# Attention and a feed-forward network on one core: the value products of eight more pairs on 64x64 quarters, in another place of the order

## The chip, the core and the metric

The kernel runs on one core of a Trainium2 chip. The core has a matrix engine (TensorE, PE in the profile, with a separate row PEld for its weight loads), a vector engine (VectorE, DVE), a scalar engine (ScalarE, ACT), GpSimd (POOL) and SyncE (SP), which here only issues DMAs. Each engine works through its own list of instructions in order, and semaphores tie the lists together. The time is the device time of one launch in microseconds (us). The kernel before takes 794.22 us, the median of 3 runs (794.18 to 794.61).

## What is computed

First attention within chunks of 64 tokens, for 8 batches, 8 heads, 576 tokens and a head width of 64; then a feed-forward layer over all 4608 tokens of width 512, with an inner width of 2048:

```python
q_c, k_c, v_c = (t.reshape(B, H, nc, 64, D) for t in (q, k, v))
scores = np.matmul(q_c, k_c.transpose(0, 1, 2, 4, 3)) / np.sqrt(D)
attn = np.exp(scores - np.max(scores, axis=-1, keepdims=True))
attn = attn / (np.sum(attn, axis=-1, keepdims=True) + 1e-09)
x = np.matmul(attn, v_c)   # then transposed to (4608, 512)
h = x @ w_in               # (4608, 2048)
out = (h - np.tanh(h)) @ w_out
```

## The kernel before

The tokens are worked through in 36 pairs of 64-token chunks, p = 0 to 35, each with its 8 heads. Four pairs (512 tokens) make a group of the feed-forward layer; there are nine groups, g = 0 to 8. All float32 numbers are split into a high and a low part, so that a product is three matmuls (high by high, high by low, low by high). From group 1 on the parts are float16.

For a pair p of 8 or more the attention is a chain through all engines. SP loads query and key (`load`) and the values (`load_values`, into one of four places of `rawv`, p % 4). DVE takes the largest value (`largest`, "tops" in the rows), POOL reduces it over partitions once a group, and a power of two follows. ACT and DVE then write the values' high and low float16 part (`split_high` L349, `split_low` L353). PE makes the scores as 16 matmuls of 64x64 (`scores`, `quarters` L183); DVE takes their maximum and subtracts it (`less` L374, L378), ACT the exponential, DVE the sum and the shares, which are split (L405, L410) and turned by a DMA transpose (`turned` L415). PE multiplies the turned shares by the values (`products`). `results` writes the outcome into the input of the feed-forward layer, 3 steps for an even p and 9 for an odd one: first ACT copies the accumulator out (L450), then ACT and DVE make sums and differences (L460 to L465) and their high and low parts (L454).

Products have two forms here. For p = 8 to 15 the values stand block-diagonally in tiles padded with zeros, and `products` runs 24 matmuls with a 128x128 weight tile (L440) into the second of two accumulator banks. For p = 16 and more `crossed_products` runs 48 matmuls of 64x64 on the four quarters of the array (L427), into the upper halves of both banks. Padded tiles exist in two places, p % 2. `two_banks` gives a new accumulator pair each time (there is one buffer) until `third`; after that one pair, `att.banks`, is kept, and its first bank is also the feed-forward bank Z.

The feed-forward layer of groups 2 and later uses a scheme with 7 products for 8 (`Winograd`). Its first matrix product is made in banks X, Y and Z (`product`, L687, 12 matmuls of 128x256 each), each result goes through ACT and DVE (`copied`, `summed` L709, `tanh` L713, `less` L717, `high` L723, `low` L727) and becomes a chunk g of two float16 halves. The second matrix product takes one chunk at a time (`chunk` L746, 12 matmuls of 128x512). The third matmul of a chunk is the first that reads the low half. The same holds for groups 0 and 1 with `gemm1` (L575), `tanh`, `less`, `high`, `low` (L584 to L608) and `gemm2` (L620).

The order is written out by hand for all engines in two tables of tokens, PLAN and SECOND. SECOND covers pairs 8 to 15 and groups 1 and 2. Its tokens that matter here: S8 is the scores of pair 8, m its `less`, E its exponentials, z, h, l its shares and their parts, t its transpose, s and d the split of its values, V8 its products, X8.0 to X8.8 the steps of `results`, u its `largest`. G and P are `gemm1` and `gemm2`, K5 is chunk 5 of group 2, gx, gy, gz and so on are products into banks X, Y, Z, and st, sn, su, sh, sl are `summed` to `low`. From group 3 on only PE's order is given by hand (the loops at the end of the function: scores of pair p + 1 directly behind the products of p); a scheduler places the other engines' work and may place it ahead of the last instructions of SECOND. In the text below K14 is the third chunk that PE works off after the scores of pair 16.

Of the kernel before, what the change touches and what calls it, by code (L numbers as in the profile page):

```python
# [10 lines left out]
F32 = mybir.dt.float32  # L11
# [5 lines left out]
AF = mybir.ActivationFunctionType  # L17
ALU = mybir.AluOpType
# [14 lines left out]
FIRST = tuple(sum(SIZES[:g]) for g in range(len(SIZES)))  # L33
# [28 lines left out]
CROSSED = FIRST[LATER + 1]  # L62

@with_exitstack
def attn_ffn_kernel(ctx: ExitStack, tc: tile.TileContext, qkE, vE, qL, kL, vL, w_in, w_out, out):
# [212 lines left out]
    class Late:  # L278
# [2 lines left out]


        def __init__(self, pool):
            self.pool, self.st, self.banks = pool, defaultdict(dict), None

            self.rawv = pool.tile([P, MOST // P, H * CH], F32, name="rawv", bufs=1)
            self.v16, self.a, self.aT, self.blocks = [], [], [], []
            self.room([pool.tile([P, 2, DM], F16, name=f"v16{a}", bufs=1).rearrange("p a n -> p (a n)") for a in "hl"])

        def two_banks(self):  # L290

            return ps_a.tile([P, 2, 4 * P], F32, name="psa") if self.banks is None else self.banks

        def room(self, v):

            self.v16.append([t.rearrange("p (c hp d) -> p c hp d", c=2, hp=4) for t in v])
            for t in v:
                nc.gpsimd.memset(t, 0.0)

        def load(self, p):  # L300
            if p < NPAIR:
# [27 lines left out]
            power(self.st[f"g{g}"]["across"], to, back)  # L329
            to_x[g], from_x[g] = to, back  # L330

        def crossed(self, p):
            return p >= CROSSED

        def split_parts(self, p):
            to = to_x[p // 4]
            if self.crossed(p):
                vh, vl = (t.rearrange("p c hp d -> p (c hp d)")[:, :DM] for t in self.v16[p % len(self.v16)])
                yield vh, vl, self.rawv[:, p % 4], to
                return  # L340
            v = self.rawv[:, p % 4].rearrange("p (a d) -> p a d", d=D)
            vh, vl = (t.rearrange("p c hp d -> p (c hp) d") for t in self.v16[p % len(self.v16)])
            for u in range(2):
                r = slice(u * D, (u + 1) * D)
                yield vh[r, :, r], vl[r, :, r], v[r], to[r]

        def split_high(self, p):
            for h, l, v, to in self.split_parts(p):
                nc.scalar.activation(h, v, AF.Copy, scale=to)  # L349

        def split_low(self, p):
            for h, l, v, to in self.split_parts(p):
                nc.vector.scalar_tensor_tensor(out=l, in0=v, scalar=to, in1=h, op0=ALU.mult, op1=ALU.subtract)  # L353

        def split(self, p):
            self.split_high(p)
# [73 lines left out]
        def products(self, p):  # L430
            if self.crossed(p):
                return self.crossed_products(p)
            d = self.st[p]
            bank = d["bank"] = self.two_banks()[:, 1]
            ps = bank.rearrange("p (hp c k) -> p hp c k", hp=4, c=2)
            for hp in range(4):
                for c in range(2):
                    cs = slice(c * CH, (c + 1) * CH)
                    for k, (a, b) in enumerate(((0, 0), (0, 1), (1, 0))):
                        nc.tensor.matmul(ps[:, hp, c, :], lhsT=self.v16[p % len(self.v16)][a][:, c, hp, :], rhs=d["a16"][:, b, hp, cs], start=(k == 0), stop=(k == 2))  # L440

        def results(self, p, x):

# [2 lines left out]
            cs = slice(p % 4 // 2 * P, (p % 4 // 2 + 1) * P)  # L446

            def out(to):
                flat = to.rearrange("p s k (c t) -> p (s k) c t", c=2) if self.crossed(p) else to.rearrange("p s k n -> p (s k n)")
                return lambda: nc.scalar.mul(flat, bank, 2.0 ** -14)  # L450

            def parts(slot, a):
                h, l = (t[:, slot:slot + a.shape[1], :, cs] for t in x)
# [572 lines left out]
```

## Time and profile before

The profile is one execution that took 793.73 us, of which the span of the engines' work is 792.0 us. The median of the timed runs is 794.22 us.

| engine | busy us | share | instructions |
|---|---|---|---|
| PE (matmul) | 784.5 | 99% | 7178 |
| PE (weight load) | 519.5 | 66% | 7178 |
| DVE | 610.8 | 77% | 1114 |
| ACT | 485.3 | 61% | 938 |
| POOL | 47.9 | 6% | 82 |

The granted clock of PE is at nine tenths or more of full speed in all of the 40 slices of the span. DVE's busy share is nine tenths in the slices from the second to the thirteenth (some 20 to 257 us) and six to eight tenths in most of the later ones. The chain that ended last lies with PE for 88% of the span. Busy matmuls overlap, since each is printed with its way through the array; what a matmul costs PE is the distance from its start to the next start. In the same way a DVE or ACT instruction starts some 0.08 us before the printed end of the one ahead if it needs nothing from it. Pairs 8 to 15 are worked on between 130 and 285 us; the groups from 3 on begin at 291 us.

### The profile page before, as it was taken

Reading aid. Unit: us, or ns where it says so; the run is one execution under the profiler, and the core shown is the slowest. Engines: PE = TensorE matmul, PEld = TensorE weight load, DVE = VectorE, ACT = ScalarE, POOL = GpSimd, SP = SyncE. Lnnn points to the kernel's source line nnn. Section 1 sums busy time; section 2 is a strip of 40 time slices with the busy share of each in tenths; the row PEclk is TensorE's granted clock in tenths of the full one; section 3 lists DMA queues with packets and bytes.
Section 4 is the critical chain, followed back from the end, with each engine's and each line's share of the span. In section 5 each row is a group of like instructions: output and inputs, shape, how many; then the busy total and the mean of one; then the engine's idle time right before and its main releaser. Section 6 shows DMA issues by size and latency. Waiting matters only on the chain.

```text
span 792.0 us, 17323 instructions
## 1 busy us (share of the span) xinstructions
PE 784.5 (99%) x7178; PEld 519.5 (66%) x7178; DVE 610.8 (77%) x1114; ACT 485.3 (61%) x938; POOL 47.9 (6%) x82
## 2 busy tenths in 40 slices
PE   8999999999999999999999999999999999999998
PEld 4877884444676666666666666666666666666664
DVE  8999999999999997676867686768676777654443
ACT  6989968986675655555645465556455645453443
POOL 0032135500000000000000000000000000000000
PEclk9999999999999999999999999999999999999999
DMA  9887848853131224111311131112211220001001
GB/s 355 321 234 220 222 130 179 150 134 81 28 111 50 81 61 108 47 55 54 108 55 54 55 105 37 50 40 92 68 55 41 68 67 15 15 12 43 1 1 54
DMA packets 58735, 72.43 MB, mean 91 GB/s; under 512 B 32800, under 2 KB 33056, under 8 KB 58528
## 3 DMA queue, kind: packets, MB, share of 16 engines
q1 hardware_dynamic: 53760, 61.81, 24.8%
q0 software_dynamic: 4752, 9.44, 7.0%
q8 instruction: 56, 0.92, 0.5%
q14 instruction: 23, 0.19, 0.1%
q10 hardware_dynamic: 144, 0.07, 0.0%
HBM read 45.09 MB, written 9.44 MB: 69 GB/s over the span
## 4 chain that ended last, share of the span: by engine, by line
PE 88%; DVE 7%; ACT 2%; DMA 2%; issue 1%; SPq 0%; DVEq 0%; ACTq 0%
PE po L746 36%; PE ph L687 23%; PE psa L687 9%; PE po L620 7%; PE ph L575 7%; PE psa L183 2%; PE psa L427 1%; DVE w L153 1%; DVE w L157 1%; DMA raw<-w_out 1%; PE psa L440 1%; DVE wl L164 1%; ACT junk L168 1%; DMA raw<-w_in 1%; DVE w L149 1%
## 5 line engine op out<-in xcount | busy, mean ns | idle before, releaser
L746 PE MATMUL po<-wl,gh 128*128 128x512 f16 x672 | 154.2, 379 | 0.0
L746 PE MATMUL po<-wl,gl 128*128 128x512 f16 (+1 forms) x672 | 151.6, 375 | 0.0
L687 PEld LDWEIGHTS <-wh 128*128 128x128 f16 x1344 | 129.2, 98 | 22.3
L687 PE MATMUL ph<-xh,wl 128*128 128x256 f16 x672 | 114.6, 273 | 0.0
L746 PEld LDWEIGHTS <-gl 128*128 128x128 f16 x720 | 69.1, 98 | 67.3
L687 PEld LDWEIGHTS <-wl 128*128 128x128 f16 x1008 | 98.5, 98 | 21.6
L746 PEld LDWEIGHTS <-gh 128*128 128x128 f16 x672 | 65.7, 98 | 67.3
L687 PE MATMUL ph<-xl,wl 128*128 128x256 f16 x336 | 91.6, 273 | 0.0
L687 PE MATMUL ph<-xh,wh 128*128 128x256 f16 x448 | 76.7, 273 | 0.0
L687 PE MATMUL psa<-xh,wh 128*128 128x256 f16 x448 | 76.4, 273 | 0.0
L620 PE MATMUL po<-wl,gh 128*128 128x512 f16 (+1 forms) x192 | 63.2, 383 | 0.0
L687 PE MATMUL ph<-xl,wh 128*128 128x256 f16 x224 | 61.1, 273 | 0.0
L687 PE MATMUL psa<-xl,wh 128*128 128x256 f16 x224 | 61.0, 273 | 0.0
L713 ACT ACTIVATE t<-t,sig 128x512 f32<-128x512 f32 x37 | 26.6, 719 | 32.9 <-DVE t L709 32.8
L713 ACT ACTIVATE t<-wh,sig 128x512 f32<-128x512 f32 x38 | 27.3, 720 | 31.0 <-DVE wh L709 30.9
L713 ACT ACTIVATE t<-spare,sig 128x512 f32<-128x512 f32 x37 | 26.6, 720 | 30.0 <-DVE spare L709 30.0
L575 PE MATMUL ph<-xl,wl 128*128 128x512 f16 x192 | 43.8, 379 | 0.2 <-DVE t L591 0.2
L454 ACT CAST xh<-wh 128x512 f16<-128x512 f32 (+1 forms) x56 | 31.4, 564 | 11.1 <-DVE wh L461 9.9
L709 DVE TENSOR_TENSOR wh<-ph,wh 128x512 f32<-128x512 f32 x28 | 19.3, 688 | 24.3 <-PE ph L687 24.1
L709 DVE TENSOR_TENSOR t<-ph,t 128x512 f32<-128x512 f32 x28 | 19.2, 687 | 23.4 <-PE ph L687 23.3
L387 ACT ACTIVATE s<-s 128x512 f32<-128x512 f32 x24 | 15.1, 629 | 36.0 <-DVE s L378 36.0
L717 DVE SCALAR_TENSOR_TENSOR wh<-wh,sig,t 128x512 f32<-128x512 f32 x38 | 28.4, 748 | 11.1 <-ACT t L713 11.0
(181 smaller groups left out, 1444.3 us busy)
## 6 DMA issues: line engine op xcount, KB each, us to landing
raw<-w_in SPq DMA_DIRECT2D x16, 512.0 KB, 6.0
raw<-w_out SPq DMA_DIRECT2D x16, 512.0 KB, 6.7
wh<-wl POOLq DMA_DIRECT2D x32, 256.0 KB, 4.2
rawv<-vL SPq DMA_DIRECT2D x28, 256.0 KB, 3.1
rawq<-qL SPq DMA_DIRECT2D x28, 256.0 KB, 3.1
rawk<-kL SPq DMA_DIRECT2D x28, 256.0 KB, 3.5
out<-wh SPq DMA_DIRECT2D x28, 256.0 KB, 2.1
qk<-qkE SPq DMA_DIRECT2D x8, 512.0 KB, 8.7
```

The costliest lines, as they stand in the source:

```text
L149: nc.vector.tensor_single_scalar(w, w, 3, op=ALU.logical_shift_left)
L153: nc.vector.scalar_tensor_tensor(out=w, in0=low, scalar=29, in1=w, op0=ALU.logical_shift_right, op1=ALU.bitwise_or)
L183: nc.tensor.matmul(ps[os, r ^ o if crossed else r, hp * CH:(hp + 1) * CH], lhsT=lhsT(rs, hp, o), rhs=rhs(rs, hp, o), start=True, stop=True)
L387: nc.scalar.activation(s, s, AF.Exp, scale=scale)
L454: return (lambda: nc.scalar.copy(out=h, in_=a)), (lambda: nc.vector.tensor_sub(l, a, h))
L575: nc.tensor.matmul(ph, lhsT=self.weight(fc, 0, a)[:, kc * P:(kc + 1) * P], rhs=x[b][:, kc, cols], start=(k == 0), stop=(k == 3 * KC - 1))
L620: nc.tensor.matmul(self.po[t], lhsT=gg[a][:, ts], rhs=self.weight(fc, 1, b), start=(k == 0), stop=(k == 3 * FC - 1))
L687: nc.tensor.matmul(bank[:, q * 2 * P:(q + 1) * 2 * P], lhsT=self.weight(u, a, i, q, kc), rhs=self.x[j][:, b, kc, :], start=(first and q == ...
L709: nc.vector.tensor_tensor(out=c, in0=self.banks["X"], in1=self.m5 if n % 4 == 3 else c, op=ALU.subtract if n % 4 == 2 else ALU.add)
L713: nc.scalar.activation(t, self.now[n][0], AF.Tanh, scale=self.ff.sig)
L717: nc.vector.scalar_tensor_tensor(out=c, in0=c, scalar=self.ff.sig, in1=t, op0=ALU.mult, op1=ALU.subtract)
L746: nc.tensor.matmul(bank, lhsT=g[a][:, ts], rhs=half_w[1][fc][:, b, columns], start=(first and s == 0 and k == 0), stop=(last and s == 1 an ...
```

## The change

Pairs 8 to 15 use the 64x64 form, too: the padded form, its two zero fills per pair of tiles on POOL and the distinction between the forms go. The split values lie unpadded, so that one tile holds two pairs, and there are four places, p % 4, instead of two. `split_high` and `split_low` are one instruction of 128 partitions each where pairs 8 to 15 had two of 64. In SECOND each V stands directly ahead of the scores of the pair two further on (V8 S10, V9 S11, V11 S12, V12 S13, to V15 S16), V10 stands alone, and the first step of the results (X.0) behind that. The products leave their accumulator pair to the scores that follow (`shared`). The scores and the layout of the values in memory are rearranged to match.

```diff
-... z8 ... T0.3.1 T0.2.0 V8 G8 T0.3.0 ... q10 X8.0 i8 ... C1.12 S10 G2 P10 t9 ...
+... z8 ... T0.3.1 T0.2.0 G8 T0.3.0 ... q10 i8 ... C1.12 V8 S10 X8.0 G2 P10 t9 ...
...
-... rB4 sl11 su12 X13.6 V15 gv3 X14.2 X15.0 X15.1 sh12 st13 ... K11 S16 su13 ...
+... rB4 sl11 su12 X13.6 gv3 X14.2 sh12 st13 gw3 sn13 K11 V15 S16 X15.0 su13 ...
...
         def two_banks(self):
-            return ps_a.tile([P, 2, 4 * P], F32, name="psa") if self.banks is None else self.banks
+            if self.banks is not None:
+                return self.banks
+            t, self.shared = self.shared, None
+            return ps_a.tile([P, 2, 4 * P], F32, name="psa") if t is None else t
         def room(self, v):
-            self.v16.append([t.rearrange("p (c hp d) -> p c hp d", c=2, hp=4) for t in v])
-            for t in v:
-                nc.gpsimd.memset(t, 0.0)
+            self.v16 += zip(*(t.rearrange("p (n k) -> n p k", n=2) for t in v))
...
         def split_parts(self, p):
...
+            return (*self.v16[p % 4], self.rawv[:, p % 4], to_x[p // 4])
...
+        def products(self, p):
+            d = self.st[p]
+            self.shared = None
+            tile_ = self.two_banks()
+            if self.banks is None:
+                self.shared = tile_
+            ps = tile_[:, :, 4 * CH:]
+            v = [t.rearrange("p (c hp d) -> p c hp d", c=2, hp=4) for t in self.v16[p % 4]]
...
-    turned[:, :, CROSSED:, 1] = turned[:, ::-1, CROSSED:, 1]
+    turned[:, :, :, 1] = turned[:, ::-1, :, 1]
```

Three places of the engines' lists show what moves. Line numbers of the changed kernel are smaller by 1 to 21. The first is DVE where pair 15 ends and group 3 begins, from the split of the values of pair 17 on, before:

```order
L353 SCALAR_TENSOR_TENSOR wh_1813<-rawv,to,wh_1812 128x512
L460 TENSOR_TENSOR wh_2168<-wh_2167,wh_2166 128x256
L461 TENSOR_TENSOR wh_2168<-wh_2167,wh_2168 128x256
L709 TENSOR_TENSOR spare<-ph,spare 128x512
L464 TENSOR_TENSOR wh_2169<-wh_2167 128x256
L465 TENSOR_TENSOR wh_2169<-wh_2168,wh_2166 128x256
L454 TENSOR_TENSOR xl<-wh_2168,xh 128x4x128
L717 SCALAR_TENSOR_TENSOR spare<-spare,sig,t 128x512
L727 SCALAR_TENSOR_TENSOR gh<-wh_2713,to_g,gh 128x512
L454 TENSOR_TENSOR xl<-wh_2169,xh 128x4x128
L727 SCALAR_TENSOR_TENSOR gl<-spare,to_g,gl 128x512
L315 TENSOR_REDUCE tops<-rawv 128x1
```

The same place now (the first two rows split pairs 17 and 18, the sixth pair 19; the two L706 rows are the low halves of chunks 12 and 13):

```order
L341 SCALAR_TENSOR_TENSOR v16l<-rawv,to,v16h 128x512
L341 SCALAR_TENSOR_TENSOR wh_1811<-rawv,to,wh_1810 128x512
L696 SCALAR_TENSOR_TENSOR spare<-spare,sig,t 128x512
L706 SCALAR_TENSOR_TENSOR gh<-wh_2794,to_g,gh 128x512
L315 TENSOR_REDUCE tops<-rawv 128x1 x3
L341 SCALAR_TENSOR_TENSOR wh_1811<-rawv,to,wh_1810 128x512
L439 TENSOR_TENSOR wh_2222<-wh_2221,wh_2220 128x256
L440 TENSOR_TENSOR wh_2222<-wh_2221,wh_2222 128x256
L443 TENSOR_TENSOR wh_2223<-wh_2221 128x256
L444 TENSOR_TENSOR wh_2223<-wh_2222,wh_2220 128x256
L706 SCALAR_TENSOR_TENSOR gl<-spare,to_g,gl 128x512
L315 TENSOR_REDUCE tops<-rawv 128x1
```

With four places the scheduler splits pairs 18 and 19 here too, and takes the largest values of pairs 20 to 23 where it took those of 20 and 21. The split of pair 19 uses the place that V15 reads. The sums of pair 15 (L460 to L465 before, L439 to L444 now) have moved from ahead of the two low halves to between them; the remaining rows of group 2 and of the softmax of pair 16 follow behind.

The second place is DVE where pair 11 ends and group 2 begins, before (L608 is the low half for P12, L374 and L378 belong to the softmax of pair 12, L460 to L454 to the results of pair 11):

```order
L460 TENSOR_TENSOR wh_2168<-wh_2167,wh_2166 128x256
L461 TENSOR_TENSOR wh_2168<-wh_2167,wh_2168 128x256
L608 SCALAR_TENSOR_TENSOR gl<-t,to_g,gh 128x512
L374 TENSOR_REDUCE mx<-psa 128x8
L378 TENSOR_TENSOR s<-psa,mx 128x512
L454 TENSOR_TENSOR xl<-wh_2168,xh 128x4x128
```

And the same place now:

```order
L587 SCALAR_TENSOR_TENSOR gl<-t,to_g,gh 128x512
L362 TENSOR_REDUCE mx<-psa 128x8
L366 TENSOR_TENSOR s<-psa,mx 128x512
L439 TENSOR_TENSOR wh_2222<-wh_2221,wh_2220 128x256
L440 TENSOR_TENSOR wh_2222<-wh_2221,wh_2222 128x256
L433 TENSOR_TENSOR xl<-wh_2222,xh 128x4x128
```

The two sums of pair 11 have gone behind the softmax steps, directly ahead of the row (L433) that needs ACT's high part of these sums.

The third place is ACT around the first step of the results of pair 13 (L450, now L429), before:

```order
L723 ACTIVATE gl<-wh_2713,to_g 128x512
L450 ACTIVATE wh_2167<-psa 128x512
L723 ACTIVATE gh<-spare,to_g 128x512
L510 ACTIVATE wh_3098<-wh_2908,to_w 128x512
L713 ACTIVATE t<-t,sig 128x512
```

And now:

```order
L702 ACTIVATE gl<-wh_2794,to_g 128x512
L702 ACTIVATE gh<-spare,to_g 128x512
L489 ACTIVATE wh_3172<-wh_3011,to_w 128x512
L692 ACTIVATE t<-t,sig 128x512
L429 ACTIVATE wh_2221<-psa 128x512
```

The copy out of the accumulator has gone three instructions later, as V13 itself has gone behind a whole chunk on PE.

## Rows read from the trace of the kernel before

**Rows 1.** Who PE waited for, 133 to 792 us: total, times, longest
```profile
PE ph L575 <- DVE t L591: 0.2, 1, 0.2
```

**Rows 2.** Busy time 222 to 285 us: length, PE, PEld, DVE, ACT, POOL; clock, DMA
```profile
222.00:285.00 63.00, 63.00 (x568) 42.37 (x566) 61.07 (x114) 42.30 (x71) 0.79 (x1) 1.00 0.26 76
```

**Rows 3.** PE in order of time at V9 (padded): start, us, line, form
```profile
175.12 0.86 PE L440 MATMUL psa<-s,wh 128*128 128x64 f16 x24
175.82 0.60 PE L620 MATMUL po<-wl,gh 128*128 128x512 f16 x2
```

**Rows 4.** PE in order of time, pair 16: products on quarters, scores, next product
```profile
304.15 0.26 PE L427 MATMUL psa<-wh,v16h 64*64 64x64 f16 x8
...
304.60 0.69 PE L183 MATMUL psa<-rawk,rawq 64*64 64x64 f32 x32
305.23 0.39 PE L687 MATMUL ph<-xh,wh 128*128 128x256 f16 x2
```

**Rows 5.** DVE in order of time, from the sums of pair 11 on
```profile
203.26 0.42 DVE L460 TENSOR_TENSOR wh<-wh,wh 128x256 f32<-128x256 f32 x1
...
204.06 0.75 DVE L608 SCALAR_TENSOR_TENSOR gl<-t,to_g,gh 128x512 f16<-128x512 f32 x1
204.72 0.68 DVE L374 TENSOR_REDUCE mx<-psa 128x8 f32<-128x512 f32 x1
...
206.65 0.15 DVE L123 TENSOR_REDUCE from<-xtop 128x1 f32<-128x4 f32 x1
...
211.30 0.75 DVE L608 SCALAR_TENSOR_TENSOR gl<-t,to_g,gh 128x512 f16<-128x512 f32 x1
```

**Rows 6.** PE in order of time: end of S12, and P11
```profile
204.57 0.60 PE L620 MATMUL po<-wl,gh 128*128 128x512 f16 x2
...
212.38 0.59 PE L620 MATMUL po<-wl,gh 128*128 128x512 f16 x2
```

**Rows 7.** DVE in order of time: softmax of pair 14, low half of chunk 5
```profile
242.89 0.68 DVE L374 TENSOR_REDUCE mx<-psa 128x8 f32<-128x512 f32 x1
...
247.84 0.74 DVE L727 SCALAR_TENSOR_TENSOR gl<-t,to_g,gl 128x512 f16<-128x512 f32 x1
```

**Rows 8.** PE in order of time: S14 and K5
```profile
241.97 0.69 PE L183 MATMUL psa<-rawk,rawq 64*64 64x64 f32 x32
...
249.13 1.24 PE L746 MATMUL po<-wl,gl 128*128 128x512 f16 x5
```

**Rows 9.** PE in order of time: behind V15, second product, S16, K14
```profile
278.59 0.38 PE L687 MATMUL ph<-xh,wh 128*128 128x256 f16 x2
...
279.90 0.38 PE L687 MATMUL ph<-xh,wl 128*128 128x256 f16 x2
...
283.89 0.69 PE L183 MATMUL psa<-rawk,rawq 64*64 64x64 f32 x32
...
294.95 2.75 PE L746 MATMUL po<-wl,gh 128*128 128x512 f16 x12
```

**Rows 10.** ACT in order of time: split of pair 17, a high part
```profile
278.67 0.72 ACT L349 ACTIVATE wh<-rawv,to 128x512 f16<-128x512 f32 x1 [1.05 <-PE psa L440]
...
281.01 0.62 ACT L454 CAST xh<-wh 128x512 f16<-128x512 f32 x1 [0.23 <-DVE wh L461]
```

**Rows 11.** DVE in order of time: tops, maximum, sum of pair 16, low half of chunk 14
```profile
285.35 0.68 DVE L315 TENSOR_REDUCE tops<-rawv 128x1 f32<-128x512 f32 x1
285.95 0.68 DVE L374 TENSOR_REDUCE mx<-psa 128x8 f32<-128x512 f32 x1
...
289.26 0.68 DVE L393 TENSOR_REDUCE sm<-s 128x8 f32<-128x512 f32 x1
...
292.95 0.75 DVE L727 SCALAR_TENSOR_TENSOR gh<-t,to_g,gh 128x512 f16<-128x512 f32 x1
```

**Rows 12.** DMA issues, 279 to 284 us: queue, count, KB each, us to landing
```profile
rawv<-vL SPq DMA_DIRECT2D x2, 256.0 KB, 2.7
```

**Rows 13.** Line L308 (value loads), whole span: us from issue to landing
```profile
DMA to landing us min/median/max: 2.4/3.1/5.0
```

More of the change, by code (lines that the diff above doesn't have):

```diff
@@ new lines @@
+v8 0i12 v9 W0.2 wA v11 0j12 x 0k12 0P14 xA 0G11 v10 0i11 0q12 wB 0P12 0j11 xB C0.0 W1.4 W1.8 W1.7 0k11 Cx1 C1.0 Cx0 0q11 f D0.0 Dx1 0P11 C1.6 Dx0 C0.1 G0 C0.3 D0.1 G1 D1.0 C1.3 e1 C1.5 C1.1 i0 D0.3 j0 C0.2 e0 D1.1 k0 C0.9 a8 C0.6 e2 G3 o1 u11 e3 q0 o0 W0.13 W0.10 P0 u10 u9 a9 i3 D0.6 i1 W1.10 j3 j1 k1 C0.5 u8 D1.6 q1 G6 C1.8 C1.7 W0.7 W0.8 k3 i6 D0.5 D1.3 C1.10 P1 M D0.9 C0.10 S8 o2 D1.5 W1.2 a10 G9 C1.9 j6 k6 C0.7 rA2 q3 P3 D1.10 i9 m8 D1.7 q6 E8 G5 C1.4 C0.13 j9 D0.2 P6 D0.7 k9 G7 C0.8 D1.9 W0.4 W1.13 W1.15 z8 rB2 T0.0.0 T0.0.1 D1.8 i5 q9 j5 W0.14 h8 C1.2 k5 T0.1.1 D0.10 D0.8 C0.4 l8 T0.1.0 C1.13 s8 t8 i7 W1.14 W0.15 s9 D1.2 S9 D1.13 T0.2.1 j7 m9 C0.14 q5 d8 fb P9 D0.13 G10 P5 k7 E9 z9 T0.3.1 T0.2.0 G8 T0.3.0 i10 h9 j10 q7 D1.4 D0.4 P7 W0.12 s10 k10 q10 i8 C1.14 C0.15 l9 c0.1 c0.2 d10 j8 D0.15 W1.12 W0.11 C0.12 C1.12 V8 S10 X8.0 G2 P10 t9 k8 i2 m10 b0.2 E10 q8 c0.0 D0.14 d9 G4 j2 k2 b0.1 z10 P8 D1.12 X8.1 i4 a12 j4 q2 c0.3 h10 a11 D1.14 G13 b0.0 s11 C1.15 l10 V9 S11 X9.0 i13 b0.3 v14 X9.1 m11 X9.4 T1.0.0 P2 X8.2 D0.12 o3 v13 T1.0.1 T1.2.1 X9.2 t10 X9.5 k4 q4 E11 W1.11 G15 i15 z11 X9.6 C1.11 d11 P4 j13 C0.11 v15 h11 l11 X9.7 k13 j15 V10 G14 i14 q13 k15 v12 P13 D1.15 t11 G12 X10.0 u15 u12 T1.1.0 D0.11 j14 D1.11 k14 q15 X9.3 u13 X9.8 i12 X10.1 T1.2.0 X10.2 T1.3.0 T1.1.1 q14 T1.3.1 P15 j12 k12 c1.3 u14 rA3 G11 V11 S12 X11.0 q12 m12 X11.1 X11.5 X11.2 P14 i11 a13 P12 E12 X11.3 rB3 c1.2 z12 j11 X11.4 gz0 s12 h12 k11 c1.0 X11.6 l12 gy0 q11 P11 t12 c1.1 sc0 mc0 ee2 b1.3 b1.0 b1.2 d12 b1.1 gx0 gu0 ee0 X11.7 ee3 st0 sn0 X11.8 oo2 oo3 T2.0.1 su0 ee1 oo1 gv0 sc1 a14 st1 gw0 sh0 T2.1.1 V12 S13 X12.0 sl0 gq0 sc2 T2.3.1 K0 m13 sn1 s14 st2 su1 sn2 sh1 gz1 su2 E13 sl1 z13 X12.1 h13 T2.2.1 st3 gy1 l13 sh2 T2.0.0 t13 sc4 d14 oo0 mc1 K1 s13 gx1 T2.2.0 sl2 sn3 T2.1.0 gu1 st4 T2.3.0 d13 sc5 K2 su3 X12.2 v18 sn4 c2.2 su4 gv1 sh3 sl3 sh4 c2.3 st5 gw1 sn5 sl4 K3 V13 S14 X13.0 c2.0 b2.2 c2.1 b2.3 v17 su5 X13.1 b2.0 gq1 m14 K4 sc6 v16 X13.2 E14 sh5 st6 b2.1 z14 st7 h14 sl5 l14 gz2 mc2 sn6 t14 gy2 a15 K5 u18 T3.0.0 su6 sn7 T3.1.0 T3.0.1 sh6 sc8 X13.4 T3.3.0 T3.1.1 sl6 T3.3.1 u16 gx2 T3.2.1 su7 st8 gu2 s15 u17 T3.2.0 sh7 K6 gv2 sn8 su8 gw2 sc9 c3.0 sl7 sh8 d15 c3.2 sc10 K7 st9 b3.0 c3.1 v19 sl8 V14 S15 X14.0 gq2 sn9 c3.3 K8 X14.1 b3.1 su9 m15 st10 b3.2 gz3 sh9 sl9 st11 sn10 E15 z15 h15 sn11 su10 l15 b3.3 u19 su11 a16 gy3 K9 sc12 mc3 sh10 t15 X13.3 X13.7 rA4 sl10 gx3 gu3 sh11 st12 X13.8 sc13 X13.5 sn12 K10 rB4 sl11 su12 X13.6 gv3 X14.2 sh12 st13 gw3 sn13 K11 V15 S16 X15.0 su13 gq3 sh13 sl12 X15.1 X15.2 X15.4 X15.5 sc14 sl13 st14 X15.3 X15.7 st15 m16 X15.6 X15.8 E16 K12 z16 sn14 sn15 su14 h16 sh14 su15 sh15 K13 a18 l16 sl14 sl15 t16 a17
@@ L61 @@
 SUMMED = (8, 9, 10, 11)
-CROSSED = FIRST[LATER + 1]
 @with_exitstack
@@ L330, in powers_of_tops @@
             to_x[g], from_x[g] = to, back
-        def crossed(self, p):
-            return p >= CROSSED
         def split_parts(self, p):
[L336 to L345, printed above, removed]
+            return (*self.v16[p % 4], self.rawv[:, p % 4], to_x[p // 4])
         def split_high(self, p):
-            for h, l, v, to in self.split_parts(p):
-                nc.scalar.activation(h, v, AF.Copy, scale=to)
+            h, l, v, to = self.split_parts(p)
+            nc.scalar.activation(h, v, AF.Copy, scale=to)
         def split_low(self, p):
-            for h, l, v, to in self.split_parts(p):
-                nc.vector.scalar_tensor_tensor(out=l, in0=v, scalar=to, in1=h, op0=ALU.mult, op1=ALU.subtract)
+            h, l, v, to = self.split_parts(p)
+            nc.vector.scalar_tensor_tensor(out=l, in0=v, scalar=to, in1=h, op0=ALU.mult, op1=ALU.subtract)
         def split(self, p):
@@ L428, in crossed_products @@
             d["bank"] = ps.rearrange("p c (hp k) -> p hp c k", hp=4)
[L430 to L440, printed above, removed]
         def results(self, p, x):
@@ L448, in out @@
             def out(to):
-                flat = to.rearrange("p s k (c t) -> p (s k) c t", c=2) if self.crossed(p) else to.rearrange("p s k n -> p (s k n)")
-                return lambda: nc.scalar.mul(flat, bank, 2.0 ** -14)
+                return lambda: nc.scalar.mul(to.rearrange("p s k (c t) -> p (s k) c t", c=2), bank, 2.0 ** -14)
             def parts(slot, a):
```

8 lines of the change are left out of this document (2 added, 6 removed).

## The prediction

> **What bounds the kernel now.** I read the page's shares first: PE is busy for 99% of the span, so the question is whether PE ever waits. The view of waits says that from 133 us on it waited 0.2 us in all [rows 1]: a microsecond taken from PE's own list is a microsecond of the time, and one that PE has to wait is added to it. Then the busy times by stretch: from 222 to 285 us PE is busy for 63.00 of 63 us, DVE for 61.07 [rows 2]. The reader is to see two saturated engines, of which PE just leads. DVE has nothing to make up a delay with, and the change touches both. So I set the new lists of DVE and ACT against the times of the old ones and asked at each matmul that reads DVE's last step which of the two comes first.
>
> **PE's own work.** A padded pass takes 0.70 us (175.12 to 175.82) [rows 3], the same products on quarters 0.45 (304.15 to 304.60) [rows 4]. That is 0.25 for each of the seven pairs whose products stand directly ahead of scores; the scores cost the same, 0.63 [rows 4], and their change to 64x64 and back is paid today. V10 stands alone and pays this change itself; it can save 0 to 0.25, and I take 0.1. Sum: 7 x 0.25 + 0.1 = 1.85 us less, with bounds of 1.75 and 2.0.
> The Trainium skill's page "TensorEngine Tiling (Array Packing)", section "Key Properties", says that a change of tiling mode drains the engine, which speaks against V10's place. By the rule V10 saves nothing and the sum is 1.75; the 0.1 is not needed for any step below.
>
> **What costs nothing.** The split of a pair loses one instruction on DVE and one on ACT, at most the 0.75 and 0.72 us of a full one [rows 10, 11], eight times. PE waits for none of them, so I count nothing; it is room for DVE before each of the places below, where DVE starts behind PE or ACT anyhow. If DVE's room counted in full, it would be up to 0.75 at a place. The zero fills go from POOL, which is busy for 0.79 of 63 us [rows 2]; what stood behind them, the additions of weight parts, comes earlier, and nobody waits for it [rows 1]. V12 to V15 now use the half of bank Z that only scores used; the scores directly behind them wait for the same readers today, so nothing new. The copy X.0 of an accumulator must be done before the next V; a whole round of chunks lies between. On SP the transposes of shares may leave a microsecond later, with many microseconds to their V. All of these: 0.
>
> **Three places where DVE comes late.** In each I count from the end of a PE step to the moment at which DVE has written the low half, and to PE's third matmul behind, the first that reads it. A chunk's matmuls follow each other every 0.215 us, so the third is 0.43 behind the first.
>
> P11. Before, S12 ends at 204.57 and P11 starts at 212.38 [rows 6]; its third matmul is 7.81 + 0.43 = 8.24 behind S12. PE's list between the two is unchanged. DVE took up the maximum of pair 12 0.15 behind S12 (204.72) and the low half 6.58 later (211.30) [rows 5]. Now the two sums of pair 11 (203.26 to 204.06, 0.80 [rows 5]) stand inside this stretch, and the next row needs ACT's high part of them, 0.62 [rows 10] and some 0.16 for the last write and two handovers, in which DVE stands still: 0.78. So the low half is written 0.15 + 6.58 + 0.80 + 0.78 + 0.75 = 9.06 behind S12. PE waits 0.8. Bounds: 0 (if DVE has enough room ahead to take the sums elsewhere, which its list does not allow but the order of arrival might hide) and 1.5 (the exponential of pair 12, now behind that high part on ACT, comes late by its own 0.6 too).
>
> K5. Before, S14 starts at 241.97 and K5 at 249.13 [rows 8]; with the third matmul 7.59. V13 now ends where S14 starts. ACT's copy of V13's result takes about 0.1 and 0.6 us (a similar ACT row has 0.62 [rows 10]), the two sums 0.80 [rows 5], a weight conversion between them and the maximum 0.66 (204.06 to 204.72 for the same kind of step [rows 5]), and from the maximum of pair 14 to the low half of chunk 5 it is 4.95 (242.89 to 247.84), and 0.74 to write it [rows 7]: 7.85. PE waits 0.26, against nothing before, where the sums did not wait for V13. Bounds 0 and 0.8.
>
> K14. This is the large one. V15 now ends where S16 starts, and from there it is 283.89 to 294.95 and 0.43, 11.49 us, to the third matmul of K14 [rows 9]. In this time DVE must do what the new list puts there:
> - The split of pair 19 waits for V15's place, for ACT's half of it (0.1 and 0.72 [rows 10]), and in DVE's list it stands behind the largest value of pair 22, whose load can be issued only when pair 18 is split. Two products and a chunk lie between the old V15 and S16, 5.30 us (278.59 to 283.89), the first product 1.31 of it [rows 9]. In the new list V15 follows them: it ends 5.30 + 0.45 = 5.75 behind the first product's start. The step that reads the first product starts at 1.31 + 0.15, then come 0.60 [rows 11] and two splits of 0.66: pair 18 is written at 3.46, 2.29 ahead of V15's end. The load takes 0.05 and 2.7 [rows 12], the largest value 0.60: the split of pair 19 starts 1.1 behind V15's end.
> - Behind it: the split 0.66, two pairs of sums 0.80 and 0.70, the low half of chunk 13 0.66: to 3.9. Then DVE takes the largest value of pair 23, whose load follows the split of pair 19: 1.1 + 0.75 + 0.05 + 2.7 = 4.6. DVE stands still for 0.7.
> - From 4.6: four steps of 0.60 [rows 11] (that largest value, two sums of the feed-forward layer, a low part), 2.4; maximum, scaling, subtraction, 0.68 + 0.1 + 0.6; two low parts 0.34 + 0.6; then from the sum of pair 16 to the low half of chunk 14 as before, 3.69, and 0.75 [rows 11]; between them the power of two of group 5, 0.64 (206.65 to 207.29, where the next step starts: I take 0.5, as it falls into the gaps of the small softmax steps) [rows 5]. End: 4.6 + 2.4 + 1.38 + 0.94 + 3.69 + 0.75 + 0.5 = 14.3.
> PE waits 14.3 - 11.5 = 2.8 to 2.9. Bounds: without the two loads the split starts at 0.84 and nothing stands still, 13.3, a wait of 1.9; with loads of 5.0 [rows 13] it is 3.5 for the split, 9.3 for the last load, 19.0 in all, a wait of 7.6. I take 2.9, since the 2.7 is of loads into the same tile at this place. Before, the same low half was ready at 293.70 and K14's third matmul came at 295.38 [rows 9, 11].
>
> Sum against the profiled execution: 793.73 - 1.85 + 0.8 + 0.26 + 2.9 = 795.84 (span 794.1). The median of the timed runs is 0.49 above that execution, so in their scale 794.22 + 2.1 = 796.3.
>
> **Rivals.** (1) PE alone: none of the three waits appears, since DVE runs far enough ahead. For it: PE waits for nothing today [rows 1], and eight steps of 0.75 go from DVE. Against: 61.07 of 63 us [rows 2], and DVE cannot run ahead of V15, whose result it needs. It gives 794.22 - 1.85 = 792.4, faster. It decides if the low half of chunk 14 is written within 11.5 us of V15's end. The Trainium skill's page "Perfetto Trace Analysis", section "Identifying the Most-Contended Engine", says to optimize the engine of the highest occupancy first; that is PE, and by it the whole 1.85 would come out.
> (2) The loads of pairs 22 and 23 are no obstacle and P11 and K5 just hold: only 1.9 at K14 is left, 794.3, no change. For it: the 0.8 and 0.26 are smaller than what I can add up over ten steps. Against: both loads depend on splits that stand right ahead.
> (3) The loads take the longest time seen: 7.6 at K14, 801. Against: the queue is quiet there.
>
> **How the numbers follow.** A measurement of this kernel can tell 0.2%, 1.6 us, from no change: faster is below 792.6, slower above 795.8. Forecast 0.62, with its own range 795.2 to 797.8, of which a seventh (0.09) lies below 795.8; (1) 0.14, (2) 0.19, (3) 0.05. Slower 0.53 + 0.05 = 0.58, same 0.19 + 0.09 = 0.28, faster 0.14. The range of 793.2 to 798.4 leaves out (1) and (3).
>
> **What would show it.** In the new profile: products of pairs 8 to 15 at 0.45 us; a PE wait at K14 (line of `chunk`) for DVE's `low` of 2 to 3.5 us, with DVE standing still ahead of a largest value for the load of pair 23; waits under 1 us at P11 and K5; no other. Wrong if PE's waits sum to less than 1.9 us, or if a V itself waits.

## The result and the profile after

The changed kernel takes 799.31 us, the median of 6 runs, against 794.04 of the kernel before: 1.0065 times as long, with an interval of 1.0051 to 1.0079, so 4 to 6 us slower. One of the 6 runs, of 2869.55 us, is left out of the ratio; the other five lie between 798.34 and 800.90 us. The forecast was 796.3 and its range ended at 798.4. The direction is right, the size is not: +5.3 where +2.1 was forecast.

The profiled execution took 798.44 us, with a span of 796.6 (792.0 before). The waits of PE in it from 133 us on, in the view of [rows 1]:

```profile
PE po L725 <- ACT gh L702: 2.2, 1, 2.2
PE po L599 <- DVE gl L587: 1.2, 2, 0.8
PE po L725 <- DVE gl L706: 0.8, 1, 0.8
PE po L725 <- DVE gh L706: 0.6, 1, 0.6
PE po L599 <- ACT gh L578: 0.3, 1, 0.3
```

Before there was one wait of 0.2. This view counts from the printed end of a matmul, which overlaps the next, so it is up to 0.2 short per wait. Below a wait is counted from starts: the distance from a step's first matmul to the next step's, less what the step takes undisturbed (2.59 for 12 matmuls of 512 columns, 1.31 for 12 of 256).

DVE in the stretch of [rows 2] is less busy than before, 56.73 us instead of 61.07:

```profile
222.00:285.00 63.00, 62.09 (x616) 40.99 (x601) 56.73 (x110) 38.67 (x65) 0.79 (x1) 1.00 0.26 76
```

It has not got room: it stands still for 5.3 us in this stretch (0.8 before), since what it needs comes later. In the profile before, DVE's share stays at nine tenths up to the fifteenth slice, to 297 us, so K14 lies in the stretch of a full DVE, too.

PE's own work, V11 with S12 behind it, and V10 alone with the last matmul ahead of it and the first behind (answers to [rows 3, 4]):

```profile
203.33 0.58 PE L419 MATMUL psa<-s,wh 64*64 64x64 f16 x48
203.78 0.69 PE L182 MATMUL psa<-rawk,rawq 64*64 64x64 f32 x32
...
189.46 0.38 PE L599 MATMUL po<-wl,gl 128*128 128x512 f16 x1
189.77 0.57 PE L419 MATMUL psa<-s,wh 64*64 64x64 f16 x48
190.28 1.04 PE L554 MATMUL ph<-xl,wl 128*128 128x512 f16 x4
```

V11 costs 0.45 where 0.70 stood. V10 costs 0.51, and the matmul ahead of it 0.31 instead of 0.22, so 0.10 is saved there.

P11 (answers to [rows 5, 6]), PE, then DVE, then ACT from the end of S12 at 204.41 on:

```profile
212.11 0.27 PE L666 MATMUL ph<-xl,wl 128*128 128x256 f16 x1
212.68 0.60 PE L599 MATMUL po<-wl,gh 128*128 128x512 f16 x2 [0.30 <-ACT gh L578]
214.14 0.39 PE L599 MATMUL po<-wl,gl 128*128 128x512 f16 x1 [0.85 <-DVE gl L587]
```

```profile
205.17 0.69 DVE L362 TENSOR_REDUCE mx<-psa 128x8 f32<-128x512 f32 x1 [1.03 <-ACT wh L429]
205.89 0.69 DVE L366 TENSOR_TENSOR s<-psa,mx 128x512 f32<-128x512 f32 x1
206.50 0.42 DVE L439 TENSOR_TENSOR wh<-wh,wh 128x256 f32<-128x256 f32 x1
...
208.06 0.69 DVE L433 TENSOR_TENSOR xl<-wh,xh 128x512 f16<-128x512 f32 x1 [0.68 <-ACT xh L433]
...
213.33 0.75 DVE L587 SCALAR_TENSOR_TENSOR gl<-t,to_g,gh 128x512 f16<-128x512 f32 x1
```

```profile
204.53 0.60 ACT L429 ACTIVATE wh<-psa 128x512 f32<-128x512 f32 x1 [0.59 <-PE psa L182]
```

The reader is to see three things. The copy X11.0 (L429) starts 0.12 behind the end of the scores, not of V11, and was released by the scores' line (L182). The maximum of pair 12 (L362) was released by that copy and starts 0.76 behind S12; before it was 0.15. And DVE stands still for the high part, 0.68 from the printed end and 0.77 by starts, where 0.78 was forecast. PE waits 0.46 at the start of P11 and 1.03 inside it.

K5 (answers to [rows 7, 8]):

```profile
249.96 0.59 PE L725 MATMUL po<-wl,gl 128*128 128x512 f16 x2
251.40 2.33 PE L725 MATMUL po<-wl,gl 128*128 128x512 f16 x10 [0.84 <-DVE gl L706]
```

```profile
244.19 0.43 DVE L439 TENSOR_TENSOR wh<-wh,wh 128x256 f32<-128x256 f32 x1 [2.29 <-ACT wh L429]
...
245.65 0.68 DVE L362 TENSOR_REDUCE mx<-psa 128x8 f32<-128x512 f32 x1
...
250.60 0.74 DVE L706 SCALAR_TENSOR_TENSOR gl<-t,to_g,gl 128x512 f16<-128x512 f32 x1
```

```profile
243.56 0.60 ACT L429 ACTIVATE wh<-psa 128x512 f32<-128x512 f32 x1 [3.49 <-PE psa L182]
```

V13 ends at 242.80, S14 at 243.43; the copy starts at 243.56. PE waits 1.01.

K14 (answers to [rows 9, 11, 12]): on PE the product ahead of it, K14 itself and the product behind; on DVE the two stops for loads (of pairs 21 and 23), between them the split of pair 19, and the low half.

```profile
295.36 0.38 PE L666 MATMUL psa<-xh,wh 128*128 128x256 f16 x2
...
299.01 0.61 PE L725 MATMUL po<-wl,gh 128*128 128x512 f16 x2 [2.17 <-ACT gh L702]
300.18 2.33 PE L725 MATMUL po<-wl,gh 128*128 128x512 f16 x10 [0.57 <-DVE gh L706]
302.35 0.38 PE L666 MATMUL psa<-xh,wh 128*128 128x256 f16 x2
```

```profile
286.37 1.36 DVE L315 TENSOR_REDUCE tops<-rawv 128x1 f32<-128x512 f32 x2 [0.25 <-DMA rawv<-vL]
287.65 0.74 DVE L341 SCALAR_TENSOR_TENSOR wh<-rawv,to,wh 128x512 f16<-128x512 f32 x1
...
291.03 0.69 DVE L315 TENSOR_REDUCE tops<-rawv 128x1 f32<-128x512 f32 x1 [0.51 <-DMA rawv<-vL]
...
299.38 0.75 DVE L706 SCALAR_TENSOR_TENSOR gh<-t,to_g,gh 128x512 f16<-128x512 f32 x1
```

The product takes 1.31 and K14 starts 3.65 behind it, a wait of 2.33 (for the high half, which ACT writes directly ahead of DVE's low half); K14 lasts 3.34 instead of 2.59, another 0.75. In all 3.08.

The account, from S8 to V16, in us:

| term | forecast | profile after |
|---|---|---|
| PE's own work | -1.85 | -1.84 |
| chunk ahead of V10 (P4) | 0 | 0.55 |
| P11 | 0.8 | 1.49 |
| K5 | 0.26 | 1.01 |
| K10 and K13 | 0 | 0.36 |
| K14 | 2.9 | 3.08 |
| sum | 2.1 | 4.65 |

That is the 4.6 by which the span grew, and 798.44 is what this execution took. The median lies another 0.87 above it. The mean granted clock of the five runs goes with it: 1.000 in those of 798.34 and 798.44 us, 0.998 in 799.02 and 799.60, 0.996 in 800.90. The experiments show at which place the clock can fall.

### The profile page after: what moved, and what is told of

It is laid out like the page before. It is cut to its first block, busy times and chain, and to the rows that moved or that the text cites. A ratio compares the mean times of both kernels' runs of the same rounds, so it can differ in the third digit from the quotient of the medians.

```text
span 796.6 us, 17670 instructions
## 1 busy us (share of the span) xinstructions
PE 783.0 (98%) x7370; PEld 516.4 (65%) x7370; DVE 603.9 (76%) x1106; ACT 479.1 (60%) x930; POOL 44.4 (6%) x78
## 4 chain that ended last, share of the span: by engine, by line
PE 82%; DVE 11%; DMA 3%; ACT 2%; issue 1%; SPq 0%; DVEq 0%; ACTq 0%
PE po L725 34%; PE ph L666 22%; PE psa L666 8%; PE ph L554 6%; PE po L599 6%; PE psa L182 2%; DMA raw<-w_out 2%; PE psa L419 2%; DVE w L152 1%; DVE w L156 1%; ACT junk L167 1%; DVE wl L163 1%; ACT w L144 1%; DVE w L148 1%; DVE xl L433 0%
## 5 line engine op out<-in xcount | busy, mean ns | idle before, releaser
L692 ACT ACTIVATE t<-t,sig 128x512 f32<-128x512 f32 x37 | 26.6, 719 | 33.3 <-DVE t L688 33.3
L692 ACT ACTIVATE t<-wh,sig 128x512 f32<-128x512 f32 x38 | 27.3, 719 | 30.4 <-DVE wh L688 30.4
L692 ACT ACTIVATE t<-spare,sig 128x512 f32<-128x512 f32 x37 | 26.6, 720 | 28.9 <-DVE spare L688 28.9
L433 ACT CAST xh<-wh 128x512 f16<-128x512 f32 (+1 forms) x56 | 31.5, 566 | 13.8 <-DVE wh L440 12.6
L688 DVE TENSOR_TENSOR spare<-ph,spare 128x512 f32<-128x512 f32 x28 | 19.3, 688 | 23.5 <-PE ph L666 23.3
```

Of the source, the lines that this page charges most:

```text
L433: return (lambda: nc.scalar.copy(out=h, in_=a)), (lambda: nc.vector.tensor_sub(l, a, h))
L688: nc.vector.tensor_tensor(out=c, in0=self.banks["X"], in1=self.m5 if n % 4 == 3 else c, op=ALU.subtract if n % 4 == 2 else ALU.add)
L692: nc.scalar.activation(t, self.now[n][0], AF.Tanh, scale=self.ff.sig)
```

## The experiments

All times are medians; the kernel before, run beside them, took 794.0 to 794.1 us each time.

**The old order.** The new form of V, but SECOND as before, with two places (e1) and with four (e2).

```diff
-... G8 ... C1.12 V8 S10 X8.0 ... K11 V15 S16 X15.0 ...
+... V8 G8 ... X8.0 ... C1.12 S10 ... V15 gv3 X14.2 X15.0 X15.1 ... K11 S16 ...
-            return (*self.v16[p % 4], self.rawv[:, p % 4], to_x[p // 4])
+            return (*self.v16[p % 2], self.rawv[:, p % 4], to_x[p // 4])    # e1 alone
```

In both, V12 and V14 write into half of bank Z before its product has been copied out, so these values are lost; no instruction is left out.

> The changed kernel with the order of the kernel before (every V at its old place, X.0 as before) and two places for the split values. Theory (the loss comes from the order and the four places alone): no wait of PE beyond the 0.2 us of before; each of eight V is 0.19 us shorter alone (0.508 against 0.699), at most 1.5 us in all; 792.5 to 793.3. Rival (the quarter form or the unpadded split costs by itself, or the four places do not matter): 796 or more.

> As the run before, but with four places, so that the splits of pairs 18 and 19 and the largest values of pairs 22 and 23 go ahead of K14. Theory (early splits and late V15 together make the wait at K14): the added 4 steps of 0.6 to 0.66 us and the power of two 0.6, 3.1 us, against 1.7 us of room that K14 had: a wait of 0.5 to 1.5 us, 793.3 to 794.5. Rival A (the places alone make the wait): K14 waits 3 us, 796. Rival B (the late V15 alone): no wait, as the run before.

e1 took 793.13 us (ratio 0.9988, 0.9979 to 0.9997), with no wait of PE behind 133 us. From V8 to V16 its PE needs 142.61 us where 143.41 stood before: eight V alone save 0.10 each, as V10 does in the changed kernel. The expectation had 0.19 each as the upper end; the 0.09 goes to the matmul ahead. So neither the form nor the unpadded split costs anything. e2 took 793.70 (0.9996, 0.9987 to 1.0004), and PE waits 0.75 at K14 by starts, part of it at the next product's bank:

```profile
PE po L725 <- DVE gh L706: 0.3, 1, 0.3
PE psa L666 <- ACT m L658: 0.2, 1, 0.2
```

The four places alone cost some 0.6 to 0.75 us. Both theories of one cause for K14's 3 us fall.

**V15 alone early (e3).**

```diff
-... X13.6 gv3 X14.2 sh12 ... K11 V15 S16 X15.0 su13 gq3 sh13 sl12 X15.1 ...
+... X13.6 V15 gv3 X14.2 X15.0 X15.1 sh12 ... K11 S16 su13 gq3 sh13 sl12 ...
```

> The changed kernel with V15, X15.0 and X15.1 alone back at their old places. Theory: P11 and K5 wait as in the changed kernel (1.5 and 1.0 us), K14 waits 0.5 to 1.5 us in place of 3.1, and V15 loses 0.2 us of its gain: 797 to 798. Rival A (places alone): K14 still waits 3 us, 799.5. Rival B (V15 alone): no wait at K14, 796.3.

797.25 us (1.0040, 1.0027 to 1.0052). P11 and K5 wait as in the changed kernel, K14 1.81 instead of 3.08. So of K14's wait 1.3 us comes from the late V15 and what is queued behind it. Some 0.75 come with the four places in any order; the last 1.1 this run does not place (if the parts add up).

**Scores brought forward to the values, everywhere but at pair 12 (e4),** two places. As above, V14's early place loses values of bank Z.

```diff
-... G8 ... C1.12 V8 S10 X8.0 ...
+... V8 S10 G8 ... X8.0 ... C1.12 a11 ...
```

> V and S stand together as in the changed kernel, but at the old place of V (the scores come forward, V12 excepted, which stays ahead of S13), and with two places. Theory (what costs is that the results come later, not that V and S stand together): PE gains 1.85 us as in the changed kernel, the copy of the accumulator comes 0.4 us later than in the kernel before, PE waits 0 to 0.6 us: 792.2 to 792.8. Rival (V directly ahead of S costs by itself, since the copy waits for the scores and the maximum for the copy): waits at P11 and K5 of 0.6 us or more each remain, 793.5 or more.

793.15 us (0.9990, 0.9981 to 0.9999). Neither theory as it stood: at P11 and K5 there is no wait, but 0.57 and 0.55 appear at the two chunks behind the early S16, K12 and K14. DVE had the largest value of pair 20 there, two sums behind the splits, and stood still 1.76 us for its load. At P11 and K5 the scores may stand at V; pair 15 is better left alone.

**What the copy waits for (e5).** In the changed kernel the product gq1 goes between V13 and S14, and the copy directly behind V13.

```diff
-... K3 V13 S14 X13.0 ... b2.0 gq1 m14 ...
+... K3 V13 X13.0 gq1 S14 ... b2.0 m14 ...
```

> The changed kernel with one edit: behind V13 stands X13.0 and the product gq1 (1.3 us on PE), and S14 behind that, instead of V13 S14 X13.0 and gq1. Theory (K5 waits 1.0 us instead of the 0.26 forecast because the copy X13.0 does not start when V13 ends but when the scores directly behind it end, 0.63 us later): the copy now starts within 0.2 us of V13's end and K5 waits 0.2 to 0.5 us, while V13 alone costs PE 0.15 to 0.2 more: 0.3 to 0.7 us faster than the changed kernel. Rival (DVE is late by work handed on from the waits before, P11 above all): K5 still waits 1.0 us.

```profile
242.92 0.60 ACT L429 ACTIVATE wh<-psa 128x512 f32<-128x512 f32 x1 [2.93 <-PE psa L419]
```

```profile
250.05 3.05 PE L725 MATMUL po<-wl,gl 128*128 128x512 f16 x12
```

V13 ends at 242.78 here. The copy starts 0.14 behind it, released by V's own line (L419), and K5's 12 matmuls last 3.05 where an undisturbed chunk prints 2.75 [rows 9]; by starts the wait is 0.29, against 1.01. So at K5 it is the copy, not work handed on. The time did not follow, though: 799.70 us (1.0069, 1.0056 to 1.0081). K13 waits 0.71 us now in place of 0.11, since DVE stands still for 0.82 and not 0.25 for the load of pair 21:

```profile
286.30 1.39 DVE L315 TENSOR_REDUCE tops<-rawv 128x1 f32<-128x512 f32 x2 [0.82 <-DMA rawv<-vL]
```

That and V13 alone (0.15) take back the 0.72 of K5; the one run at a full mean clock took 798.30, where those of the changed kernel stand. And behind K14's wait the profiled execution shows this, from 299.50 to 303.50, e5 first and then the changed kernel (last columns: granted clock, DMA share, GB/s):

```profile
299.50:303.50 4.00, 3.43 (x10) 1.26 (x10) 2.30 (x8) 1.80 (x4) 0.00 (x0) 0.57 0.69 173
```

```profile
299.50:303.50 4.00, 3.43 (x22) 2.03 (x22) 2.99 (x8) 2.70 (x6) 0.00 (x0) 1.00 0.71 169
```

PE works on 10 matmuls instead of 22 in this time: after the wait the clock fell to its lower level, 1.2 instead of 2.4 GHz (0.50 from 299.75 to 303.00), and K14 lasts 4.83 us instead of 3.34. This loss strikes some executions and not others (K14 lasts 4.47 in e6 and 4.89 in e9, but 3.34 in e11). That it is the scatter of the changed kernel, too, follows from the mean clocks of its runs; there is no profile of the changed kernel at the lower clock.

**The maximum first (e6).** The maximum of pair 14 ahead of the copy, the sums of pair 13 behind the low half of chunk 5.

```diff
-... V13 S14 X13.0 ... su5 X13.1 b2.0 gq1 m14 K4 sc6 v16 X13.2 ... sl5 l14 ...
+... V13 S14 ... su5 b2.0 gq1 m14 X13.0 K4 sc6 v16 ... sl5 X13.1 X13.2 l14 ...
```

> The changed kernel with the maximum of pair 14 ahead of the copy X13.0, and the sums X13.1 and the high part X13.2 behind the low half of chunk 5. Theory (in the changed kernel DVE stands still for 2.3 us ahead of K5 until the copy is done, though nothing in K5 needs the sums of pair 13): the wait at K5 goes, 1.0 us faster than the changed kernel, 798.2 where that is 799.3. Rival (DVE has too much work whatever its order): the wait stays or shows up at the next chunks, 799.

800.39 us (1.0081, 1.0067 to 1.0095): the theory is wrong here, the rival right. K5 waits 0.22, and the next chunk, K6, 1.16. DVE still stands still for 2.2 us:

```profile
243.59 0.69 DVE L362 TENSOR_REDUCE mx<-psa 128x8 f32<-128x512 f32 x1 [1.00 <-PE psa L182]
...
246.20 0.69 DVE L688 TENSOR_TENSOR wh<-ph,wh 128x512 f32<-128x512 f32 x1 [1.20 <-ACT wh L684]
```

The maximum need not wait for the copy any more, but ACT's copy waits for DVE's steps on the same accumulator, and ACT's next step (L684), which DVE needs, is queued behind that copy. The profiled execution has the lower clock behind K14, too.

**V9, V11 and V13 early, the others late (e7).**

```diff
-... V9 S11 X9.0 i13 b0.3 v14 X9.1 m11 X9.4 ... G11 V11 S12 X11.0 q12 m12 X11.1 ... K3 V13 S14 X13.0 ...
+... b0.1 V9 z10 ... a11 X9.0 D1.14 G13 b0.0 s11 X9.1 ... V11 ... G11 S12 X11.1 ... su4 V13 gv1 sh3 X13.0 ... K3 S14 ...
```

> The changed kernel with V9, V11 and V13 alone back at their old places, with their X.0, X9.1, X9.4 and X11.1; V8, V12, V14 and V15 stay directly ahead of scores and the four places stay. Theory: the waits ahead of V10 (0.55 us), around P11 (1.5) and at K5 (1.0) go, three V lose 0.15 each, K14 still waits 3 us: 796.3 to 797.3. Rival (the waits come from the eight shorter V moving the whole list forward against DVE): waits of about 3 us remain in the same stretch, 799.

796.04 us (1.0032, 1.0022 to 1.0042). The profile has these waits left:

```profile
PE po L725 <- ACT gh L702: 2.3, 1, 2.3
PE po L725 <- DVE gh L706: 0.6, 1, 0.6
```

That is K14 (3.2 by starts; K10 keeps 0.25). The waits at P4, P11 and K5, 3.05 us together, go with three V.

**The better version (e8).** The order of before with two places; the scores come forward to V at pairs 8, 9, 11 and 13, V12 goes to S13, V14 and S15 go behind sc9, V10 and V15 stay alone.

```diff
-... V8 G8 ... X8.0 ... C1.12 S10 ...
+... V8 S10 G8 ... X8.0 ... C1.12 a11 ...
-... V14 gv2 sn8 su8 gw2 sc9 c3.0 ... S15 gq2 ...
+... gv2 sn8 su8 gw2 sc9 V14 S15 c3.0 ... gq2 ...
```

> Two places and the order of the kernel before, with the scores brought forward to V at pairs 8, 9, 11 and 13; V12 stands ahead of S13, V14 and S15 behind the copy of the second product of bank Z; V10 and V15 stand alone at their old places. Theory: six V directly ahead of scores save 0.25 us each, two alone 0.1, 1.7 in all, and since no result comes later than it is needed PE waits for nothing: 792.3 (791.9 to 792.8). Rival (wherever V and S stand together, the copy behind the scores makes a wait of 0.5 us or more): 793.5 or more.

792.21 us, ratio 0.9978 (0.9969 to 0.9987), and no wait of PE behind 133 us. It is faster than both kernels, by 1.8 and 7.1 us. From S8 to V16 PE needs 163.78 us where 165.50 stood before: 1.72 of its 1.84 are to be had, with four of the pairs V and S at V's old place instead of S's, one at S's and one in between.

**Three places (e9)** in the changed kernel:

```diff
-            return (*self.v16[p % 4], self.rawv[:, p % 4], to_x[p // 4])
+            return (*self.v16[p % 3], self.rawv[:, p % 4], to_x[p // 4])
```

> The changed kernel with three places for the split values instead of four: the split of pair 19 and the largest value of pair 23 no longer go ahead of K14, V15 stays late. Theory (K14's wait is the early work of group 3 on DVE together with the load that follows V15): the stop of 0.5 us for the load of pair 23, that largest value, 0.6, and the power of two, 0.6, go: K14 waits 1.2 to 1.8 us in place of 3.1, 1.3 to 2.5 us faster than the changed kernel, 797 to 798. Rival (the sums of pair 15 behind the late V15 set K14): still 3 us, 799.3.

799.80 us (1.0068, 1.0056 to 1.0081), a miss. DVE's stops for loads:

```profile
286.65 0.69 DVE L315 TENSOR_REDUCE tops<-rawv 128x1 f32<-128x512 f32 x1 [0.75 <-DMA rawv<-vL]
...
290.52 0.69 DVE L315 TENSOR_REDUCE tops<-rawv 128x1 f32<-128x512 f32 x1 [0.40 <-DMA rawv<-vL]
```

By starts K14's own waits fall from 3.08 to 2.46, by one DVE step of 0.6 and no more: the second load that DVE stops for is now that of pair 22, and it still follows a split that waits for V15. The profiled execution has the lower clock, too (K14 lasts 4.89), which hides the 0.6.

**Four places in the better order (e10).**

```diff
-            return (*self.v16[p % 2], self.rawv[:, p % 4], to_x[p // 4])
+            return (*self.v16[p % 4], self.rawv[:, p % 4], to_x[p // 4])
```

> The order with the scores brought forward to the values (792.2 with two places), with four places. Theory: as in the order of the kernel before, four places cost 0.5 to 0.8 us at K14 and nothing elsewhere: 792.7 to 793.1. Rival (with enough room ahead of K14 the early splits cost nothing): 792.2.

792.71 us (0.9984, 0.9975 to 0.9993): 0.5 more than with two, though the two intervals overlap. The trace has 0.74 at K14, as e2 had.

**The wait filled (e11).** In the changed kernel the product ahead of K14 is made twice.

```diff
             self.product("Z", u, 3, 3, True)
+            if ff.g == LATER and u == 0:
+                self.product("Z", u, 3, 3, True)
```

> The changed kernel with the product ahead of K14 (bank Z, 12 matmuls, 1.31 us) made twice, the second time over the first, inside the 2.3 us in which PE waits there. Theory (PE's granted clock falls after that wait in some executions, to 0.50 for 3 to 4 us, and costs these 1.1 to 1.5 us; that is why the changed kernel scatters from 798.3 to 800.9): with a wait of 1.0 us the clock stays at 1.00, all runs lie at 798.2 to 798.8, 0.5 to 1 us faster in the median although PE does 1.31 us more. Rival (the scatter is from elsewhere): as the changed kernel, 799.3 with the same scatter, or 1.3 slower.

798.37 us (1.0055, 1.0043 to 1.0068), from 797.97 to 799.14: with 1.31 us more work for PE the median is 0.9 lower than the changed kernel's, and where the runs at full clock of that stood. K14 waits 0.90 and 0.75, and the granted clock of the profiled execution is 1.00 throughout. The mean clocks of its five runs are 0.999 to 1.000, against 0.996 to 1.000. But the intervals of the two ratios overlap and the runs spread further than the 798.2 to 798.8 expected, so this supports the reading and does not settle it; that the clock falls there at all, the rows in e5 show.

## Why the forecast was wrong

What held: PE's own 1.85 (1.84), that V10 saves 0.1, the places P11, K5 and K14, their order of size, and K14's mechanism. Forecast was the low half of chunk 14 at 14.3 us behind the end of V15, and it came 300.13 - 285.50 = 14.6 behind. That the two are so close is luck in part: DVE came to these splits 1.0 late (that of pair 18 was written 1.3 ahead of V15's end and not 2.29), so the split of pair 19 started 2.15 behind V15 and not 1.1, and the last load was there at 5.5 and not 4.6; the rest then took 9.1 where 9.7 was forecast. DVE stopped for two loads, 0.25 and 0.51, where 0.7 was forecast for the last. The condition of rival (1), 11.5 us, was missed by 3. Rival (2) fails, since DVE did stop for loads and P11 and K5 did wait, and rival (3) by the four loads there, which landed in 2.7 us (median). Of the signs named, two did not come: waits under 1 us at P11 and K5, and no wait elsewhere.

The step that failed is "ACT's copy of V13's result takes about 0.1 and 0.6 us", counted from where V13 ends. The copy starts 0.75 behind V, namely 0.12 behind the scores that follow, and these take 0.63. At K5 the low half came 8.54 behind V13's end where 7.85 was forecast; with the scores moved away (e5) it was 7.92. At P11 the same 0.6 sits in the maximum, which waits for the copy: the low half came 9.67 behind S12, forecast 9.06. These two places are 0.75 + 0.69 of what is missing. The trace of before shows it at another place. ACT at the last two V of the kernel before, first with scores behind V (V ends at 677.59, the scores at 678.22), then without (V ends at 698.36):

```profile
678.34 0.60 ACT L450 ACTIVATE wh<-psa 128x512 f32<-128x512 f32 x1 [1.96 <-PE psa L183]
```

```profile
698.50 0.60 ACT L450 ACTIVATE wh<-psa 128x512 f32<-128x512 f32 x1 [1.38 <-PE psa L427]
```

0.75 and 0.14 behind V. The values and the scores lie in two halves of the same two banks, the change puts them into the same form as pair 16 has, and here ACT's copy waits until PE has written both halves. The Trainium skill, page "PSUM — Partial Sum Buffer", section "PSUM bank collisions raise a hardware error", asks for such a guard: by the bank (more narrowly, the bank and 32 partitions) and not by the address, reads of two engines against each other, too. This trace agrees (0.75 against 0.14; the maximum behind the copy).

The second fault is a term put at nothing without a reason. The prediction says that it asks at each matmul that reads DVE's last step and then counts three places; P4 ahead of V10, K10 and K13 are not among them. PE at P4, then DVE behind S11 and behind S15, all in the changed kernel:

```profile
187.51 0.39 PE L599 MATMUL po<-wl,gl 128*128 128x512 f16 x1 [0.37 <-DVE gl L587]
```

```profile
182.16 0.43 DVE L439 TENSOR_TENSOR wh<-wh,wh 128x256 f32<-128x256 f32 x1 [2.18 <-ACT wh L429]
...
266.53 0.75 DVE L696 SCALAR_TENSOR_TENSOR wh<-wh,sig,t 128x512 f32<-128x512 f32 x1 [2.30 <-ACT t L692]
```

At P4 DVE stood still 2.18 us for X9.0, the same copy, and PE waited 0.55. Behind S15 the copy X14.0 delays ACT's tanh (L692), for which DVE stands still 2.30 us. Ten us later this is K10's wait. DVE's last step for K10 and K10 itself, first in the changed kernel, then in e2:

```profile
276.78 0.74 DVE L706 SCALAR_TENSOR_TENSOR gh<-spare,to_g,gh 128x512 f16<-128x512 f32 x1
```

```profile
276.91 3.00 PE L725 MATMUL po<-wl,gh 128*128 128x512 f16 x12
```

```profile
272.94 0.74 DVE L706 SCALAR_TENSOR_TENSOR gh<-spare,to_g,gh 128x512 f16<-128x512 f32 x1
```

```profile
274.89 2.75 PE L725 MATMUL po<-wl,gh 128*128 128x512 f16 x12
```

With 0.43 to the third matmul, DVE is 0.18 late in the changed kernel and 1.64 early in e2 (as in the kernel before). P4, K10 and K13 are 0.9 together.

The third is the clock. Its mean was 1.000 in the profile before, and the prediction puts a wait at its length. Behind waits of 1.5 to 2.2 us ahead of K14 it fell to its lower level in some executions (e5, e6, e9), and K14 took 1.1 to 1.6 us longer in these. In the median that is, to judge by the mean clocks, the rest: 799.31 - 798.44 = 0.87, where the kernel before has 0.3.

How K14's 3.08 divides: the four places cost 0.75 by themselves (e2, e10) and V15 early takes 1.3 off (e3). With V9, V11 and V13 early the wait is not smaller (e7, 3.2), so the rest isn't lateness carried along from those. The rows point to V14. In e7 DVE comes to the stop for the tanh with more room than in the changed kernel, and stands there longer, 2.90 us instead of 2.30:

```profile
263.55 0.75 DVE L696 SCALAR_TENSOR_TENSOR wh<-wh,sig,t 128x512 f32<-128x512 f32 x1 [2.90 <-ACT t L692]
```

So at K10 DVE is 0.2 late in the changed kernel, e3 and e7 alike, all with V14 late, and 1.6 early in e1, e2 and e8. These 1.8 us of room are enough for the 1.1 that e3 left over.

What stays open: V14 was not moved alone, so this last part is read from rows and not tried. Nor was it tried to read one half of a bank while PE writes the other.

## What to carry to other kernels

When a step of PE is put directly ahead of another that writes into the same accumulator bank, count the reader from the end of the second, and look in the trace for a pair that stands so already. Before a producer is moved back to its neighbour, try moving the neighbour forward: here the saving on PE was nearly the same (1.72 of 1.84 us), and PE waited for nothing. Where PE and DVE are both full, check every chunk of the stretch and not only the largest suspects, and reckon with the clock that may follow a PE wait as long as K14's here.

## What the runs showed of the hardware

A change between 128x128 and 64x64 work costs PE 0.15 us for going there and back: V alone takes 0.51 and the matmul ahead 0.09 more, against 0.45 where the scores follow (e1 has it eight times).

The granted clock fell from 2.4 to 1.2 GHz during K14, which stood behind a wait of 2.1 us (e5), 2.2 (e6) and 1.5 (e9); in e5 and e9 PE was in a second, shorter wait by then. It stayed at 2.4 behind 2.2 and 0.6 in the profiled execution of the changed kernel, 2.3 and 0.6 in e7, and 0.7 and 0.6 in e11.
